# Weight chunks of two matrices converted in turn, and 26 matmuls at the end of an attention and FFN kernel

## The chip, the cores and the metric

The kernel runs on one core of a Trainium2 chip. The metric is the device time of one execution in microseconds (us). The engines are named as in the profile: PE is TensorE's matmul (PEld its weight load), DVE is VectorE, ACT is ScalarE, POOL is GpSimd, and SP is SyncE, which issues the DMAs.

## What is computed

Attention over 8 batches of 8 heads, once on means of four positions and once in a band of seven positions, then a mixing of positions of rank 32, then a two-layer FFN with ReLU:

```python
def _attn_ref(q, k, v):                       # 8 x 8 x 576 x 64, float32
    factor, Sd, scale = 4, S // 4, 1.0 / np.sqrt(D)
    q_d, k_d, v_d = (t.reshape(B, H, Sd, 4, D).mean(axis=3) for t in (q, k, v))
    out_d = sm_attn(q_d, k_d, v_d)             # softmax attention on means of 4 positions
    out_up = np.repeat(out_d, factor, axis=2)
    mask = np.abs(pos[:, None] - pos[None, :]) < factor
    scores = np.where(mask, scale * np.matmul(q, k.transpose(0, 1, 3, 2)), -1000000000.0)
    ...
    out_local = np.matmul(attn, v)             # softmax over a band of 7 positions
    return out_up + out_local

def _moe_ref(x, U, V, w_ch1, w_ch2):           # x: 8 x 576 x 512, the heads side by side
    xt = x.transpose(0, 2, 1)
    h = xt @ U @ V                             # U 576 x 32, V 32 x 576
    u = x + h.transpose(0, 2, 1)
    ch = np.maximum(u @ w_ch1, 0.0) @ w_ch2    # 512 x 2048 and 2048 x 512
    return u + ch
```

The weights arrive as float64. The kernel turns each into two float32r parts, a high and a low one, and each FFN product is three matmuls (high x high, low x high, high x low).

## The kernel before

**Planner.** The whole program is one list of operations, each with an engine, a duration, a priority (a smaller number goes first), its reads and writes, and the buffers it needs. `Plan.run` walks modelled time: when an engine is free it takes the ready operation of the smallest priority number, and the order that results is the order in which instructions are issued. A buffer has a slot (a tag with so many copies) and a kind; within a kind buffers are handed out in the order in which they were created. Between kinds that share a slot the waiting operation with the smaller priority number gets the free copy.

**Attention.** A head pair is two heads of one batch; there are four for each batch and 32 in all. The priority of pair number n is 10 n, with +1 and +2 for its later stages. The first NE = 5 pairs (batch 0, and the first of batch 1) are "early": they use buffers in `early_pool`, compute the band with PE (`local_blocks`), and for batch 0 go straight on to `early_mix` (lines 617 to 638), which writes u as `uH` and `uL`. Later pairs send scores through memory, and line 711 (POOL) multiplies the values by the softmax weights of line 696 (DVE) into buffers `Pt`, which line 716 (DVE) sums; `mix_part` (lines 735 to 782) then reads the result back and makes u, with POOL writing `uL` in line 782.

**Weights.** W1 and W2 are converted in 16 chunks of 128 rows or columns each. For a chunk, SP loads 512 KB into a raw buffer (lines 376 and 385), then `convert` runs: ACT line 327, DVE lines 328, 330, 333 and 335 on a temporary `c` (three copies), ACT line 337 into the high part, POOL line 340 into the low part. Raw buffers have the tag `Pt` with kind `raw`: they share its three copies with the products `Pt` of line 711. W1 chunk f has priority 20 + 2 f (its load 5 less, and other numbers for the first three), W2 chunk f has 20 + f. W1's chunks are created first, all 16, then W2's.

**Region.** W2's tiles W2H and W2L lie where the early buffers were: `late_pool` closes `early_pool` and opens the pool of W2. The operation "late" follows all early operations, and each W2 chunk's copy into W2H waits for it.

**FFN.** 256 steps (batch, half of the positions, one of 16 chunks of the hidden layer). `ffn1` of a step is 12 matmuls of 288 columns into `ps_h` (line 799), then ACT writes `hH` (line 806) and DVE `hL` (line 807); `ffn2`, three steps later (LAG = 3), is 12 matmuls into four accumulators (line 822) from W2's chunk. The priorities are 1000 and above, so PE takes FFN work where no attention is ready. Step fc needs W1's chunk fc and W2's chunk fc, and all four head pairs of its batch. After the last chunk, POOL adds `uH` and `uL`, DVE adds the accumulator (line 835) and SP stores the result (line 838).

Of the kernel before, what the change touches and what calls it, by code (L numbers as in the profile page):

```python
# [12 lines left out]
F32R = mybir.dt.float32r  # L13
# [8 lines left out]
PE, DVE, ACT, POOL, SP = range(5)  # L22
# [31 lines left out]
class Plan:  # L54
# [9 lines left out]
    def op(self, eng, dur, fn, r=(), w=(), prio=0.0, after=(), lat=None, move=0.0, at=0.0):  # L64
        o = Op()
        o.eng, o.dur, o.fn, o.prio, o.succ, o.ndep, o.ready = eng, dur, fn, prio, [], 0, at
        o.lat, o.move = LATENCY[eng] + SLACK * (SLACK_FROM <= prio < 1000) if lat is None else lat, move
        deps = set(after)
        bufs = []
        for k in r:  # L70
            b = k[0] if isinstance(k, tuple) else k
            bufs.append(b)
            if k in self.last_w:
                deps.add(self.last_w[k])
            self.readers.setdefault(k, []).append(o)
        for k in w:
            b = k[0] if isinstance(k, tuple) else k
            bufs.append(b)
            if k in self.last_w:
                deps.add(self.last_w[k])  # L80
            deps.update(self.readers.get(k, ()))
            self.readers[k] = []
            self.last_w[k] = o
        deps.discard(o)
        o.margin = MARGIN[eng] * (MARGIN_FROM <= prio < 1000 and any(d.eng != eng for d in deps))
        o.bufs = [b for b in dict.fromkeys(bufs) if isinstance(b, Buf)]
        for b in o.bufs:
            b.uses += 1
        for d in deps:
            d.succ.append(o)  # L90
        o.ndep = len(deps)
        self.ops.append(o)
        return o
# [108 lines left out]
def attn_mix_ffn_kernel(ctx: ExitStack, tc, q, kp, vp, qT, kT, v, U, Ub, V, w1, w2, mask, band, eye, sel, pool, vw, ident, outT):  # L202
    nc = tc.nc
    B, H, S, D = q.shape
# [5 lines left out]
    DM = H * D  # L210
    DF = w1.shape[1]
    NFC = DF // 128
    NDC = DM // 128
    TN = 288
# [3 lines left out]
    LAG = 3  # L218
    W1S, W2P, W2S = 2, 20, 1
# [5 lines left out]
    W1P = 20  # L225
    NE = 5
    CN = 512
# [6 lines left out]
    op, buf = plan.op, plan.buf  # L234

    const = ctx.enter_context(tc.tile_pool(name="const", bufs=1))
# [6 lines left out]
    ps_h = ctx.enter_context(tc.tile_pool(name="ps_h", bufs=2, space=bass.MemoryType.PSUM))  # L243
    ps_m = ctx.enter_context(tc.tile_pool(name="ps_m", bufs=2, space=bass.MemoryType.PSUM))

    def psum(pool, name, tag, bufs):
        return buf(pool, [128, 512], F32, name, tag, bufs)
# [14 lines left out]
    def act(n, fn, r, w, prio, base=0.143):  # L262
        return op(ACT, n / 1200.0 + base, fn, r, w, prio)
# [11 lines left out]
    Vst = const.tile([128, S], F32R, name="Vst")  # L275
    W1H = const.tile([128, NDC, DF], F32R, name="W1H")
    W1L = const.tile([128, NDC, DF], F32R, name="W1L")
    W2 = {}
    early = tc.tile_pool(name="early", bufs=1)
    early_pool = early.__enter__()  # L280

    def late_pool():
        if not W2:
            early.__exit__(None, None, None)
            w2p = ctx.enter_context(tc.tile_pool(name="w2p", bufs=1))
            W2["H"] = w2p.tile([128, NFC, DM], F32R, name="W2H")
            W2["L"] = w2p.tile([128, NFC, DM], F32R, name="W2L")
        return W2

    def padded(shape, name, used, dt=F32):  # L290
        t = early_pool.tile([128, *shape], dt, name=name)
# [29 lines left out]
    def convert(raw, pp, n, hi_out, lo_out, a, wkey, name, prio, gate=(), l0=0):  # L321
        t = buf(ffn, [128, CN], I32, name, "cT:" + name, 3)
        w = lambda i: raw()[:pp, :2 * n].rearrange("p (n two) -> p n two", two=2)[:, :, i]
        ti = lambda: t()[:pp, :n]
        tf = lambda: t()[:pp, :n].bitcast(F32)
        ta = lambda: tf().rearrange("p (a n) -> p a n", a=a)
        act(n, lambda: nc.scalar.activation(tf(), w(1).bitcast(F32), AF.Abs), [raw], [t], prio)
        dve(n, lambda: nc.vector.tensor_scalar(
            out=tf(), in0=tf(), scalar1=F_MIN, scalar2=F_MAX, op0=ALU.max, op1=ALU.min), [t], [t], prio, True)
        dve(n, lambda: nc.vector.tensor_scalar(  # L330
            out=ti(), in0=ti(), scalar1=5, scalar2=2, op0=ALU.logical_shift_left,
            op1=ALU.logical_shift_right), [t], [t], prio, True)
        dve(n, lambda: nc.vector.scalar_tensor_tensor(
            ti(), w(1), -0x40000000, ti(), op0=ALU.bitwise_and, op1=ALU.bitwise_or), [raw, t], [t], prio)
        dve(n, lambda: nc.vector.scalar_tensor_tensor(
            ti(), w(0), 29, ti(), op0=ALU.logical_shift_right, op1=ALU.bitwise_or), [raw, t], [t], prio)
        act(n, lambda: nc.scalar.activation(hi_out(), ta(), AF.Copy), [t, *gate], [wkey + "H"], prio)
        if lo_out is None:
            return
        pool_tt(n, lambda: nc.gpsimd.tensor_tensor(  # L340
            out=lo_out(), in0=ta()[l0:], in1=hi_out()[l0:].bitcast(F32), op=ALU.subtract),
            [t, wkey + "H"], [wkey + "L"], prio)
# [31 lines left out]
    def load_w1(f, prio):  # L374
        raw = raw_buf("w1r")
        dma(lambda: nc.sync.dma_start(
            out=raw().rearrange("p (a n) -> p a n", a=NDC),
            in_=w1.bitcast(I32)[:, f * 256:(f + 1) * 256].rearrange("(a p) n -> p a n", p=128),
        ), [], [raw], min(prio - W1A, W1B + W1C * f if f < 3 else prio), 525)
        fs = slice(f * 128, (f + 1) * 128)  # L380
        convert(raw, 128, CN, lambda: W1H[:, :, fs], lambda: W1L[:, :, fs], NDC, f"W1_{f}", "c1", prio)

    def load_w2(f, prio):
        raw = raw_buf("w2r")
        dma(lambda: nc.sync.dma_start(out=raw(), in_=w2.bitcast(I32)[f * 128:(f + 1) * 128, :]),
            [], [raw], prio, 525)
        convert(raw, 128, CN, lambda: W2["H"][:, f, :].unsqueeze(1),
                lambda: W2["L"][:, f, :].unsqueeze(1), 1, f"W2_{f}", "c2", prio, ["late"])


    def work(is_early, pool, shape, dt, name, tag=None, bufs=1):
# [395 lines left out]
    FIRST, FILL = -10.0, 1000.0  # L787
# [23 lines left out]
    def ffn2(s, i):  # L811
        b, t, fc = s
        hH, hL = hbuf.pop(s)
        if fc == 0:
            accs[(b, t)] = [psum(ps_acc, f"acc{e}", f"acc{e}", 1) for e in range(NDC)]
        ac = accs[(b, t)]

        for e in range(NDC):
            def mm(e=e):
                es = slice(e * 128, (e + 1) * 128)  # L820
                for n, (w, hx) in enumerate((("H", hH), ("H", hL), ("L", hH))):
                    nc.tensor.matmul(ac[e]()[:, :TN], W2[w][:, fc, es], hx(),  # L822
                                     start=(fc == 0 and n == 0), stop=(fc == NFC - 1 and n == 2))
            op(PE, PF, mm, [hH, hL, f"W2_{fc}H", f"W2_{fc}L"], [ac[e]], FILL + i + LAG - 0.5)
        if fc == NFC - 1:
            uH, uL = u_of(b, t)
            for e in range(NDC):
                if e == NDC - 1:
                    o1 = buf(loc, [128, TN], F32, "o1", "o1b", 1)
                else:  # L830
                    o1 = buf(ffn, [128, CN], F32, "o1", "cT:o1", 3)
                pool_tt(TN, lambda e=e, o1=o1: nc.gpsimd.tensor_tensor(  # L832
                    out=o1()[:, :TN], in0=uH()[:, e, :].bitcast(F32), in1=uL()[:, e, :].bitcast(F32), op=ALU.add),
                    [(uH, e), (uL, e)], [o1], FIRST, after=[last_h[i - 1]])
                dve(TN, lambda e=e, o1=o1: nc.vector.tensor_tensor(  # L835
                    out=o1()[:, :TN], in0=ac[e]()[:, :TN], in1=o1()[:, :TN], op=ALU.add),
                    [ac[e], o1], [o1], FIRST)
                dma(lambda e=e, o1=o1: nc.sync.dma_start(
                    out=outT[e * 128:(e + 1) * 128, b * S + t * TN:b * S + (t + 1) * TN], in_=o1()[:, :TN]),
                    [o1], [], FIRST, 150, lat=0.4)  # L840

    steps = [(b, t, fc) for b in range(B) for t in range(NT) for fc in range(NFC)]
# [30 lines left out]
    held = []  # L873
    attention(1, True)
    early_ops = list(plan.ops)
    for f in range(NFC):
        load_w1(f, W1P + W1S * f)
    plan.op(DVE, 0.0, lambda: late_pool(), [], ["late"], 27, after=early_ops, lat=0.0)
    for f in range(NFC):
        load_w2(f, W2P + W2S * f)  # L880
    load_u(38)
    for h in held:
# [2 lines left out]
    for i in range(len(steps) + LAG):  # L885
        if i < len(steps):
            b, t, fc = steps[i]
            if t == 0 and fc == 0 and b > 0 and b + 1 < B:
                attention(b + 1)
            ffn1(steps[i], i)  # L890
        if i >= LAG:
            ffn2(steps[i - LAG], i - LAG)
    with tc.manual_schedule():
        plan.run()

# [61 lines left out]
```

## Time and profile before

| | us |
|---|---|
| median of 3 runs | 1093.05 |
| lowest and highest run | 1092.78, 1094.65 |
| the profiled execution | 1095.29 |
| its span in the profile | 1093.5 |

The profile is of one execution. Its span runs from the first to the last event that it recorded. "Busy" of an engine is the time in which at least one of its instructions ran; matmuls overlap, so a PE that is busy all the time need not be at its peak. PEclk is the clock granted to TensorE as a share of 2.4 GHz. In a timeline, the brackets give the idle time of the engine before the instruction and what ended it.

### The profile page before, as it was taken

Reading aid. Unit: us, or ns where it says so; the run is one execution under the profiler, and the core shown is the slowest. Engines: PE = TensorE matmul, PEld = TensorE weight load, DVE = VectorE, ACT = ScalarE, POOL = GpSimd, SP = SyncE. Lnnn points to the kernel's source line nnn. Section 1 sums busy time; section 2 is a strip of 40 time slices with the busy share of each in tenths; the row PEclk is TensorE's granted clock in tenths of the full one; section 3 lists DMA queues with packets and bytes.
Section 4 is the critical chain, followed back from the end, with each engine's and each line's share of the span. In section 5 each row is a group of like instructions: output and inputs, shape, how many; then the busy total and the mean of one; then the engine's idle time right before and its main releaser. Section 6 shows DMA issues by size and latency. Waiting matters only on the chain. (4 is left out here: it accounts for less than half of the span.)

```text
span 1093.5 us, 22919 instructions
## 1 busy us (share of the span) xinstructions
PE 1052.8 (96%) x8696; PEld 1011.7 (93%) x8696; DVE 643.8 (59%) x1093; ACT 372.8 (34%) x1239; POOL 550.0 (50%) x580
## 2 busy tenths in 40 slices
PE   7888988998999999999999999999999999999998
PEld 6777887987999999999998999999999999999998
DVE  5887899675775876745675455557366556211111
ACT  4787552333233423233242123332343221211111
POOL 4755467676575764745574534666456524202010
PEclk8898999998999999999999999999999999999999
DMA  6646864565466475543565235554656322100000
GB/s 193 190 115 181 203 191 106 139 145 140 102 163 144 112 189 129 138 96 92 124 156 125 60 102 117 137 130 109 145 126 148 79 58 75 45 1 23 1 22 23
DMA packets 238527, 125.05 MB, mean 114 GB/s; under 512 B 175632, under 2 KB 220498, under 8 KB 238416
## 3 DMA queue, kind: packets, MB, share of 16 engines
q1 hardware_dynamic: 238416, 123.58, 45.2%
q8 instruction: 69, 1.13, 0.5%
q14 instruction: 42, 0.34, 0.1%
HBM read 85.18 MB, written 38.35 MB: 113 GB/s over the span
## 5 line engine op out<-in xcount | busy, mean ns | idle before, releaser
L822 PE MATMUL acc<-hH,W2H 128*128 128x288 f32 x1024 | 316.7, 309 | 0.1
L799 PE MATMUL ps_h<-uH,W1H 128*128 128x288 f32 x1024 | 308.1, 301 | 1.4 <-DVE hL L807 1.3
L822 PE MATMUL acc<-hH,W2L 128*128 128x288 f32 x1024 | 303.5, 296 | 2.1 <-POOL W2L L340 2.1
L799 PE MATMUL ps_h<-uH,W1L 128*128 128x288 f32 x1024 | 303.3, 296 | 0.0
L822 PE MATMUL acc<-hL,W2H 128*128 128x288 f32 x1024 | 302.8, 296 | 0.0
L799 PE MATMUL ps_h<-uL,W1H 128*128 128x288 f32 x1024 | 301.2, 294 | 0.3 <-POOL uL L782 0.3
L807 DVE SCALAR_TENSOR_TENSOR hL<-ps_h,hH 128x288 fp32r<-128x288 f32 x256 | 116.1, 453 | 308.9 <-ACT hH L806 307.9
L806 ACT ACTIVATE hH<-ps_h 128x288 fp32r<-128x288 f32 x256 | 104.9, 410 | 492.8 <-PE ps_h L799 492.5
L711 POOL TENSOR_TENSOR Pt<-vl,at 128x896 f32<-128x896 f32 (+1 forms) x135 | 208.7, 1561 | 104.6 <-DVE acc L716 63.0
L716 DVE TENSOR_REDUCE acc<-Pt 128x128 f32<-128x1024 f32 (+1 forms) x135 | 242.1, 1809 | 4.4 <-DMA Pt<-up_s 2.8
L822 PEld LDWEIGHTS acc<-hH,W2H 128*128 128x128 f32 x1024 | 193.4, 189 | 8.6 <-issue 3.6
L799 PEld LDWEIGHTS ps_h<-uH,W1H 128*128 128x128 f32 x1024 | 194.2, 190 | 3.8 <-DVE hL L807 1.8
L822 PEld LDWEIGHTS acc<-hH,W2L 128*128 128x128 f32 x1024 | 193.6, 189 | 3.0 <-POOL W2L L340 3.0
L799 PEld LDWEIGHTS ps_h<-uL,W1H 128*128 128x128 f32 x1024 | 195.2, 191 | 0.6 <-POOL uL L782 0.6
L822 PEld LDWEIGHTS acc<-hL,W2H 128*128 128x128 f32 x1024 | 194.0, 189 | 0.0
L799 PEld LDWEIGHTS ps_h<-uH,W1L 128*128 128x128 f32 x1024 | 193.2, 189 | 0.0
L782 POOL TENSOR_TENSOR uL<-xT,uH 128x288 fp32r<-128x288 f32 x56 | 43.8, 806 | 102.9 <-ACT uH L780 100.2
L751 POOL TENSOR_TENSOR xL<-xL,xH 116x640 fp32r<-116x640 f32 x28 | 44.2, 1578 | 68.3 <-ACT xH L750 58.1
L832 POOL TENSOR_TENSOR o<-uH,uL 128x288 f32<-128x288 f32 x64 | 50.3, 816 | 53.1 <-DMA out_t<-o 53.0
L448 POOL TENSOR_TENSOR vr<-vr 72x256 f32<-72x256 f32 x54 | 41.7, 772 | 30.7 <-DMA vr<-in_v 30.7
L659 PE MATMUL ps_b<-gT,gq 64*96 64x102 f32 x648 | 44.3, 261 | 6.5 <-ACT se L664 3.8
L664 ACT ACTIVATE se<-ps_b 96x306 f32<-96x306 f32 x108 | 40.0, 418 | 29.5 <-PE ps_b L659 29.5
(132 smaller groups left out, 1201.9 us busy)
## 6 DMA issues: line engine op xcount, KB each, us to landing
vl<-in_vp SPq DMA_DIRECT2D x54, 240.0 KB
s_s<-se SPq DMA_DIRECT2D x108, 114.8 KB
out_t<-o SPq DMA_DIRECT2D x64, 144.0 KB
w1r<-in_W SPq DMA_DIRECT2D x16, 512.0 KB
w2r<-in_W SPq DMA_DIRECT2D x16, 512.0 KB
Y<-x_s SPq DMA_DIRECT2D x112, 72.0 KB
xL<-x_s SPq DMA_DIRECT2D x28, 287.5 KB
gT<-in_kT SPq DMA_DIRECT2D x27, 291.0 KB
```

Of the source, the lines that this page charges most:

```text
L448: pool_tt(256, lambda x=x: nc.gpsimd.tensor_tensor(out=x()[:, :, 0:2, :], in0=x()[:, :, 0:2, :], in1=x()[:, :, 2:4, :], op=ALU.add), [x], ...
L659: nc.tensor.matmul(view(ps[hh])[:, i], qr()[o, n * QB:(n + 1) * QB], kr()[o, n * QB:n * QB + KB], start=(i == 0), stop=(i == HB - 1))
L664: act(HB * KB, lambda p=ps[hh], se=se: nc.scalar.activation(se(), view(p), AF.Copy), [ps[hh]], [se], prio)
L711: nc.gpsimd.tensor_tensor(out=Pt()[:, 0:7, :n, :], in0=win, in1=at()[:, p0:p0 + n, :].rearrange("p s o -> p o s").unsqueeze(3).broadcast_t ...
L716: dve(13.7 * n * D, lambda p0=p0, n=n, Pt=Pt: nc.vector.tensor_reduce(out=acc()[:, p0:p0 + n, :], in_=Pt()[:, :, :n, :].rearrange("p o s d ...
L751: pool_tt(640, lambda: nc.gpsimd.tensor_tensor(out=xL(), in0=xL().bitcast(F32), in1=xH().bitcast(F32), op=ALU.subtract), [xL, xH], [xL], prio)
L782: pool_tt(TN, lambda uH=uH, uL=uL, uf=uf: nc.gpsimd.tensor_tensor(out=uL()[:, hp, :], in0=uf(), in1=uH()[:, hp, :].bitcast(F32), op=ALU.su ...
L799: nc.tensor.matmul(ps()[:, :TN], w[:, dc, fs], u()[:, dc, :], start=(n == 0), stop=(n == 3 * NDC - 1))
L806: last_h[i] = act(TN, lambda: nc.scalar.activation(hH(), ps()[:, :TN], AF.Relu), [ps], [hH], FIRST, 0.05)
L807: dve(TN, lambda: nc.vector.scalar_tensor_tensor(hL(), ps()[:, :TN], 0.0, hH().bitcast(F32), op0=ALU.max, op1=ALU.subtract), [ps, hH], [hL ...
L822: nc.tensor.matmul(ac[e]()[:, :TN], W2[w][:, fc, es], hx(), start=(fc == 0 and n == 0), stop=(fc == NFC - 1 and n == 2))
L832: pool_tt(TN, lambda e=e, o1=o1: nc.gpsimd.tensor_tensor(out=o1()[:, :TN], in0=uH()[:, e, :].bitcast(F32), in1=uL()[:, e, :].bitcast(F32), ...
```

## The change

Five chunks of W2 (NW = 5) get tiles of their own, `W2e`, beside the early buffers instead of in their region, and their conversions no longer wait for "late". The tiles for the other chunks become smaller by five chunks. The chunks are created in another order: W1's chunks 0 to 3, then W2's chunk 0 and W1's chunk 4 and so on in turn up to W2's chunk 4 and W1's chunk 8, then the rest of W1, then "late", then W2's chunks 5 to 15. W2's chunk f among the first five has priority 22 + 2 f; the others keep theirs. Line 822 reads W2 through `w2_of`.

At the end of the program there is a new PE operation, `widths`: 18 matmuls into one PSUM buffer, six each of 512, 384 and 128 columns, and eight of 128 columns with 64 rows of output into another. Their weights and columns are parts of W1H; nothing reads what they write. Its priority number is the largest of all.

```diff
--- before.py
+++ after.py
@@ -275,7 +275,9 @@
     Vst = const.tile([128, S], F32R, name="Vst")
     W1H = const.tile([128, NDC, DF], F32R, name="W1H")
     W1L = const.tile([128, NDC, DF], F32R, name="W1L")
+    NW = 5
     W2 = {}
+    W2e = {x: const.tile([128, NW, DM], F32R, name=f"W2e{x}") for x in "HL"}
     early = tc.tile_pool(name="early", bufs=1)
     early_pool = early.__enter__()
 
@@ -283,9 +285,12 @@
         if not W2:
             early.__exit__(None, None, None)
             w2p = ctx.enter_context(tc.tile_pool(name="w2p", bufs=1))
-            W2["H"] = w2p.tile([128, NFC, DM], F32R, name="W2H")
-            W2["L"] = w2p.tile([128, NFC, DM], F32R, name="W2L")
+            W2["H"] = w2p.tile([128, NFC - NW, DM], F32R, name="W2H")
+            W2["L"] = w2p.tile([128, NFC - NW, DM], F32R, name="W2L")
         return W2
+
+    def w2_of(x, f):
+        return W2e[x][:, f] if f < NW else W2[x][:, f - NW]
 
     def padded(shape, name, used, dt=F32):
         t = early_pool.tile([128, *shape], dt, name=name)
@@ -384,8 +389,8 @@
         raw = raw_buf("w2r")
         dma(lambda: nc.sync.dma_start(out=raw(), in_=w2.bitcast(I32)[f * 128:(f + 1) * 128, :]),
             [], [raw], prio, 525)
-        convert(raw, 128, CN, lambda: W2["H"][:, f, :].unsqueeze(1),
-                lambda: W2["L"][:, f, :].unsqueeze(1), 1, f"W2_{f}", "c2", prio, ["late"])
+        convert(raw, 128, CN, lambda: w2_of("H", f).unsqueeze(1),
+                lambda: w2_of("L", f).unsqueeze(1), 1, f"W2_{f}", "c2", prio, ["late"] if f >= NW else [])
 
 
     def work(is_early, pool, shape, dt, name, tag=None, bufs=1):
@@ -819,7 +824,7 @@
             def mm(e=e):
                 es = slice(e * 128, (e + 1) * 128)
                 for n, (w, hx) in enumerate((("H", hH), ("H", hL), ("L", hH))):
-                    nc.tensor.matmul(ac[e]()[:, :TN], W2[w][:, fc, es], hx(),
+                    nc.tensor.matmul(ac[e]()[:, :TN], w2_of(w, fc)[:, es], hx(),
                                      start=(fc == 0 and n == 0), stop=(fc == NFC - 1 and n == 2))
             op(PE, PF, mm, [hH, hL, f"W2_{fc}H", f"W2_{fc}L"], [ac[e]], FILL + i + LAG - 0.5)
         if fc == NFC - 1:
@@ -873,10 +878,15 @@
     held = []
     attention(1, True)
     early_ops = list(plan.ops)
-    for f in range(NFC):
+    for f in range(4):
+        load_w1(f, W1P + W1S * f)
+    for f in range(NW):
+        load_w2(f, W1P + W1S * f + W1S)
+        load_w1(f + 4, W1P + W1S * (f + 4))
+    for f in range(NW + 4, NFC):
         load_w1(f, W1P + W1S * f)
     plan.op(DVE, 0.0, lambda: late_pool(), [], ["late"], 27, after=early_ops, lat=0.0)
-    for f in range(NFC):
+    for f in range(NW, NFC):
         load_w2(f, W2P + W2S * f)
     load_u(38)
     for h in held:
@@ -890,6 +900,17 @@
             ffn1(steps[i], i)
         if i >= LAG:
             ffn2(steps[i - LAG], i - LAG)
+    spare = [psum(ps_h, "ps_w", "h", 2) for _ in range(2)]
+
+    def widths():
+        for k, n in enumerate([512] * 6 + [384] * 6 + [128] * 6):
+            ks = slice(k * 64, k * 64 + 128)
+            nc.tensor.matmul(spare[0]()[:, :n], W1H[:, 0, ks], W1H[:, 1, :n], start=True, stop=True)
+        for k in range(8):
+            ks = slice(k * 64, k * 64 + 64)
+            o = spare[1]()[0:64, :128]
+            nc.tensor.matmul(o, W1H[:, 2, ks], W1H[:, 3, :128], start=True, stop=True)
+    op(PE, 3.0, widths, ["W1_0H", "W1_1H", "W1_2H", "W1_3H"], spare, FILL + len(steps) + LAG)
     with tc.manual_schedule():
         plan.run()
```

## Rows read from the trace of the kernel before

**Rows 1.** The page: busy us (share of the span) and instructions of each engine

```profile
PE 1052.8 (96%) x8696; PEld 1011.7 (93%) x8696; DVE 643.8 (59%) x1093; ACT 372.8 (34%) x1239; POOL 550.0 (50%) x580
```

**Rows 2.** Stretches: length, busy us (instructions) by engine, granted PE clock, DMA share, GB/s

```profile
core 0: us, PE busy (x) PEld busy (x) DVE busy (x) ACT busy (x) POOL busy (x), PEclk, DMA share, GB/s
...
40.00:100.00 60.00, 51.82 (x483) 44.49 (x482) 45.31 (x89) 49.80 (x201) 38.37 (x41) 0.92 0.48 131
100.00:180.00 80.00, 72.83 (x565) 67.55 (x565) 73.63 (x124) 40.20 (x113) 48.90 (x45) 0.95 0.68 178
...
240.00:260.00 20.00, 13.63 (x92) 12.37 (x89) 14.75 (x22) 5.03 (x14) 14.70 (x16) 0.74 0.68 160
260.00:400.00 140.00, 139.15 (x1207) 134.20 (x1206) 96.55 (x152) 49.16 (x167) 90.28 (x96) 1.00 0.56 134
400.00:1080.00 680.00, 676.27 (x5550) 661.70 (x5549) 339.28 (x570) 184.57 (x581) 297.57 (x318) 1.00 0.38 93
```

**Rows 3.** PE timeline, 243 to 258 us: start, length, instruction, count, [idle before <-releaser]

```profile
248.86 1.23 PE L499 MATMUL ps_a<-vs,E 72*72 72x64 f32 x8 [4.61 <-POOL vs L450]
...
252.91 0.82 PE L774 MATMUL ps_u<-Vst,stk 128*128 128x288 f32 x2 [1.04 <-DVE stk L764]
...
256.50 0.61 PE L799 MATMUL ps_h<-uL,W1H 128*128 128x288 f32 x1 [0.27 <-POOL uL L782]
```

**Rows 4.** POOL timeline at the border between batch 0 and batch 1

```profile
255.65 1.55 POOL L782 TENSOR_TENSOR uL<-xT,uH 128x288 fp32r<-128x288 f32 x2 [4.64 <-ACT uH L780]
```

**Rows 5.** SP timeline, 150 to 172 us: issues of DMAs

```profile
156.76 3.81 SPq L385 DMA_DIRECT2D w2r<-in_W  x2
...
165.26 0.28 SPq L359 DMA_DIRECT2D ur<-in_U  x1
...
170.20 0.34 SPq L703 DMA_DIRECT2D Pt<-up_s  x1
```

**Rows 6.** POOL timeline: the first product of batch 1's attention

```profile
172.65 1.73 POOL L711 TENSOR_TENSOR Pt<-vl,at 128x896 f32<-128x896 f32 x1
```

**Rows 7.** DVE timeline: W2_0's last step, and line 696

```profile
108.15 1.42 DVE L335 SCALAR_TENSOR_TENSOR c<-w2r,c 128x512 int32<-128x512 int32 x1
...
119.21 0.21 DVE L696 TENSOR_TENSOR at<-ms,lrl 128x63 f32<-128x63 f32 x1
```

**Rows 8.** Tile W2H: who writes it; ns min/median/max, first and last start

```profile
L337 ACT ACTIVATE W2H<-c x16: 621/632/638, 111.8 to 175.0; 128x512 fp32r<-128x512 f32 x16
L340 POOL TENSOR_TENSOR W2L<-c,W2H x16: 1262/1310/1813, 112.8 to 175.7; 128x512 fp32r<-128x512 f32 x16
```

**Rows 9.** Chain that ended last: start, length, what

```profile
924.44 0.60 PE ps_hu L759 x10
...
1081.99 1.59 PE acc L822 x12
```

**Rows 10.** PE timeline: the first FFN matmul

```profile
103.23 0.59 PE L799 MATMUL ps_h<-uH,W1H 128*128 128x288 f32 x1
```

**Rows 11.** PE waits, 100 to 260 us: total us, times, longest

```profile
PE acc L822 <- POOL W2L L340: 2.1, 3, 1.3
```

**Rows 12.** Temporary c alone: stretch, length; DVE, ACT, POOL busy us (instructions); then as rows 2

```profile
14.00:107.00 93.00, 47.17 (x66) 20.45 (x33) 20.59 (x15) 0.87 0.59 166
107.00:178.00 71.00, 52.36 (x63) 20.00 (x32) 24.05 (x17) 0.98 0.65 170
39.00:46.00 7.00, 4.78 (x4) 2.05 (x4) 2.33 (x2) 1.00 0.69 153
```

**Rows 13.** Timeline of all engines, the end

```profile
1088.83 1.68 DVE L835 TENSOR_TENSOR o<-acc,o 128x288 f32<-128x288 f32 x4 [2.72 <-PE acc L822]
...
1089.32 1.80 SPq L838 DMA_DIRECT2D out_t<-o  x4
...
1089.66 0.29 PE L822 MATMUL acc<-hH,W2L 128*128 128x288 f32 x1
```

**Rows 14.** Stretches at the end, columns as in rows 2

```profile
1092.50:1093.50 1.00, 0.00 (x0) 0.00 (x0) 0.00 (x0) 0.00 (x0) 0.00 (x0) 1.00 0.00 0
```

## The prediction

> **What bounds the kernel now.** I read the page's engine totals first [rows 1]: TensorE (PE) is busy for 96% of the span, the next engine that computes, VectorE (DVE), for 59%. That is a modelled busy time and an average over unlike stages, so the second view is the table by stretch [rows 2]. From 260 us on, PE is busy for 139.15 of 140 and 676.27 of 680 us: there the end is set by the sum of PE work, and time saved on another engine is worth nothing. What this change wins must come from before 260 us. In 40 to 100 us ScalarE (ACT) is the fullest engine beside PE (49.80 of 60 us, DVE 45.31). In 100 to 180 us it is DVE (73.63 of 80). In 240 to 260 us PE is busy for only 13.63 of 20, at a granted clock of 0.74.
>
> Third, the PE timeline at that place [rows 3]. PE stands 4.61 us before 248.86, does small attention pieces, stands another 1.04 us, and the FFN goes on in earnest at 256.50, behind uL, which GpSimd (POOL) writes from 255.65 to 257.20 [rows 4]. This is the border between batch 0 and batch 1: the FFN waits for batch 1's attention. From there the PE work that is left is fixed, so **the kernel ends some 836 us (1093.5 - 257.2) after u of batch 1 is ready.** FFN work done sooner before the border only waits longer at it.
>
> Fourth, what sets u of batch 1. Its last three head pairs are worked off one after the other by lines 711 and 716, in Pt buffers that share three slots with the raw weight chunks. SP issues the first Pt transfer at 170.20, behind the last raw chunks (two w2r from 156.76, ur at 165.26) [rows 5], and the first product runs at 172.65 [rows 6]. The softmax result that it also reads (line 696) was there at 119.42 [rows 7]. So **the end of the weight conversions opens batch 1's attention.** From W2L's first to its last start, 112.8 to 175.7 [rows 8], the pitch is 62.9 / 15 = 4.19 us a chunk.
>
> **The change part by part.**
> *Five W2 chunks out of the early region.* Chunks 0 to 4 of W2 lose their wait on "late". In the trace W2_0 is finished in its temporary at 109.57 and copied at 111.8 [rows 7, 8], so that wait costs 2.2 us at most, once. I count it at 0: ACT may have been at other work, and the end of the conversions is set by the pitch.
>
> *The order.* Raw buffers are handed out in the order of creation: now W1_0 to W1_3, then W2_0, W1_4, W2_1, W1_5 and so on to W2_4, W1_8, then W1_9 to W1_15, then W2_5 to W2_15. The number of chunks is the same. What changes is the priority they compete with: from the fifth on it was 28, 30, ..., 50; now it is 22, 28, 24, 30, 26, 32, 28, 34, 30, 36, 38, ... So four more chunks stand ahead of the fourth early head pair (30 to 32) and five more ahead of the fifth (40 to 42). W1_9 to W1_15 are put off by up to five chunks: W1_15 is then ready near 107 + 5 x 4.19 = 128 us, while step 15 wants it no sooner than 103.23 + 15 x 3.18 = 151 us (two PE pieces of 1.59 [rows 9], FFN start [rows 10]): no stall. On SP's queue each w1r or w2r waits for a slot as before; behind them stand scores, gq and gT of the later heads, and the number of chunks ahead of these stays the same.
>
> *FFN's first steps.* W2_0 is now there when the FFN starts. But PE waited only 2.1 us for W2L in all [rows 11], and stood idle for 7.2 of 80 us in that stretch [rows 2]; what it saves there is lost again at the border. Counted at 0; if u of batch 1 were no bound it would be up to 7.2 us.
>
> *What a chunk costs in the early stage.* More chunks have a claim there, but chunks filled the gaps before as well, so I take **1.5 more chunks converted when the FFN starts**, with 0 and 4 as bounds. In 14 to 107 us a chunk took DVE 4 x 47.17 / 66 = 2.86 us and ACT 2 x 20.45 / 33 = 1.24 us [rows 12]. ACT is the fuller of the two there, so a chunk delays the early heads by 1.24 us; the other ends are 0 (it fits a gap) and 4.10 us (the heads wait for all of it in turn). Each chunk that leaves the DVE-bound stage saves 4.19 us there. Net 4.19 - 1.24 = 2.95 us, x 1.5 = **4.4 us sooner for batch 1's attention, and so for the end**. Bounds: a gain of 4 x 4.19 = 16.8 us with everything hidden; nothing with 4.10; a loss in rival (b).
>
> On DVE's price: a chunk took 2.86 us in the early stage and 4 x 52.36 / 63 = 3.32 us behind 107 us, beside other POOL work [rows 12]. The Trainium skill says in "SBUF — State Buffer" ("Who interferes with whom") that VectorE and GpSimd share one port pair by an exclusive lock, and that a VectorE operation with two SBUF inputs contends for it too; it speaks against the change, as a chunk brings its lock to the early heads' POOL work. By that a moved chunk would cost DVE 3.32 us in either stage, and with ACT 4.56, a loss of 0.4 us each; the rows of one stage do not show that, and rival (b) holds the case.
>
> *The 26 matmuls.* They come last on PE, behind the last FFN matmul at 1089.66 [rows 13]; their PSUM buffers are free since the last hL. No row has 512 columns. Scaled from 1.59 / 12 = 0.1325 us for 288 columns [rows 9], 512 take 0.236 and 384 take 0.177 us; 128 take 0.060 (ten in 0.60 us [rows 9], with weights of 64 columns, as in eight of the fourteen), at most 0.1325. Sum: 6 x 0.236 + 6 x 0.177 + 14 x 0.060 = 3.32 us, at most 4.33. They lie beside the old tail: additions on DVE until 1090.51, SP's last issue until 1091.12 [rows 13], bytes until 1092.5 at the latest [rows 14], end at 1093.5. PE ends near 1089.8 + 3.3 + 0.2 = 1093.3, at most 1094.3. If the end only needs PE to be done, that costs 0 to 0.8 us; if the same 1.0 us follows PE as follows the last bytes, 0.8 to 1.8. I take **+0.5 us**, nearer to the low end, since the transfers already end there. Less than 0 is excluded: nothing is removed from that chain.
> The Trainium skill ("TensorE: Matmul & The Clock Gate", Part 1, "Wait — 56ns, not 53.3ns?") gives for the gap of matmuls at full clock N / 2.4 GHz plus about 2.5 ns; by that estimate the 26 take 2.99 + 0.07 = 3.05 us, 0.27 less. For 288 columns it gives 122.5 ns where the row has 132.5, so I go by the row.
>
> **Sum.** -4.4 + 0.5 = -3.9 us. The profiled execution's 1095.29 becomes 1091.4; the median of the runs, 1093.05, lies 2.24 below the profiled one and becomes **1089.1 us**.
>
> **The rivals.**
> (a) *The order changes little*: no more chunks than before when the FFN starts, and only the tail is left: 1093.05 + 0.5 = 1093.6. For it: fifteen W1L ran by 107 us [rows 12], so the gaps were in use. Against: DVE idles for 14.7 of 60 us in 40 to 100 [rows 2].
> (b) *The early heads pay for it* (slower). The chunks now go ahead of the fourth and fifth head pair, on ACT and DVE in turn. One chunk beside POOL work took DVE 4.78 us in 39 to 46 us [rows 12]; with ACT's 1.24 that is 6.02. It loses from 4.19 us a chunk on. With two chunks: 2 x (6.02 - 4.19) = 3.7, and the tail 0.5: 1097.2.
> (c) *All of it fits*: four chunks at 2.95 us: -11.8 + 0.5, 1081.8. For it: DVE's idle time. Against: ACT has only 10.2 us left there.
> (d) *The border stops being a bound*, and FFN's sooner start counts: up to 7.2 us on top of (c). For it: PE's idle time at the border is 6.4 of 20 us [rows 2], which (c) would make up. Against: a sooner FFN reaches the border sooner, and waits there.
>
> **How the numbers follow.** Forecast 0.40 (1086.5 to 1091.5), (a) 0.25, (b) 0.21, (c) with (d) 0.14. The range reaches from (c) to (b): 1081.8 to 1097.5. A measurement of this kernel tells about 0.2% (2.2 us) from no change: faster is under 1090.9, slower over 1095.2. Of the forecast's 0.40, 0.36 lies under 1090.9, with (c) and (d) 0.50; (a) and the rest of the forecast make 0.29, (b) 0.21.
>
> **What would show it.** Right: W2L's last start some 4 us before 175.7, the first product before 170, the border's uL before 255, PE idle at the border as long as before or longer, the FFN's first matmul at 103 to 108, PE's last matmul ending near 1093.3. Rival (a): the same marks within 1 us of before. Rival (b): the FFN's first matmul over 8 us later than 103.23, and the first product later than 172.65. Wrong altogether: no wait of PE at the border, or several us of new PE idle time behind 260 us.

## The result, and the profile after

The changed kernel takes 1098.34 us (median of 5 runs, 1097.65 to 1099.44), the kernel before 1093.05 (1091.84 to 1094.65): a ratio of 1.0041 with an interval of 1.0029 to 1.0053. It is slower by some 0.4 to 0.5%, where 1089.1 was forecast. The profiled execution took 1097.68, its span is 1095.9. That of before was 2.24 us above its median, this one is 0.66 below, so the two traces show only 2.4 of the 5.3 us.

Line numbers from `w2_of` on are larger by 5 in the profile after. The engines' row of the page, after (compare [rows 1]):

```profile
PE 1055.8 (96%) x8722; PEld 1017.0 (93%) x8722; DVE 653.9 (60%) x1093; ACT 373.2 (34%) x1239; POOL 551.3 (50%) x580
```

The stretches of after, with the columns of [rows 2]:

```profile
40.00:100.00 60.00, 48.80 (x405) 41.81 (x403) 50.87 (x92) 45.81 (x179) 41.96 (x38) 0.83 0.49 141
100.00:180.00 80.00, 65.76 (x527) 61.54 (x528) 75.69 (x116) 42.03 (x125) 50.27 (x48) 0.89 0.61 166
180.00:240.00 60.00, 60.00 (x528) 57.66 (x527) 43.07 (x67) 20.45 (x67) 39.92 (x40) 1.00 0.66 150
240.00:260.00 20.00, 20.00 (x173) 19.10 (x172) 13.50 (x25) 8.96 (x30) 13.39 (x14) 1.00 0.70 162
260.00:400.00 140.00, 136.54 (x1134) 132.15 (x1133) 95.08 (x136) 42.40 (x137) 78.14 (x87) 0.99 0.51 125
400.00:1080.00 680.00, 679.24 (x5617) 664.54 (x5617) 345.25 (x587) 188.82 (x602) 306.46 (x327) 1.00 0.39 95
```

The reader is to see three things. PE's pause at the border is gone (20.00 of 20 us, where it was 13.63). Ahead of it PE is worse off: it is busy for 48.80 us (51.82 before) and 65.76 (72.83 before), at a lower granted clock (0.83 for 0.92, 0.89 for 0.95). Behind 260 us nothing is gained.

The FFN starts 10.3 us later than in [rows 10] (PE timeline), while batch 1's attention opens 11.0 us sooner than in [rows 6] (POOL timeline), and W2L's last start is at 168.0 where it was 175.7 in [rows 8] (tile W2L):

```profile
113.53 0.59 PE L804 MATMUL ps_h<-uH,W1H 128*128 128x288 f32 x1
```

```profile
161.62 1.83 POOL L716 TENSOR_TENSOR Pt<-vl,at 128x896 f32<-128x896 f32 x1 [1.36 <-DVE c L340]
```

```profile
L345 POOL TENSOR_TENSOR W2L<-c,W2H x11: 1279/1400/1747, 127.3 to 168.0; 128x512 fp32r<-128x512 f32 x11
```

**Where the 10.3 us arise.** The first three head pairs end as before. The fourth loses it: its softmax on ACT (`nb`, which starts it) ran at 81.20 before and at 89.74 after. ACT's timeline before, and after:

```profile
81.20 0.21 ACT L469 ACTIVATE nb<-mx 72x2 f32<-72x2 f32 x1
```

```profile
85.68 0.63 ACT L342 ACTIVATE W2eH<-c 128x512 fp32r<-128x512 f32 x1 [0.90 <-DVE c L340]
...
88.66 0.63 ACT L342 ACTIVATE W1H<-c 128x512 fp32r<-128x512 f32 x1 [0.71 <-DVE c L340]
89.20 0.64 ACT L332 ACTIVATE c<-w1r 128x512 f32<-128x512 f32 x1
89.74 0.29 ACT L474 ACTIVATE nb<-mx 72x2 f32<-72x2 f32 x2
```

The maxima that it reads came from DVE at 80.71 and 81.17 before, at 83.67 and 85.91 after, with steps of chunks between them. Then `nb` stands behind copies into W2eH and W1H, on which ACT itself sits waiting for DVE (0.90 and 0.71 us). The conversion alone (tile c) in 77 to 92 us, columns as in [rows 12], of before and of after:

```profile
77.00:92.00 15.00, 5.48 (x11) 3.15 (x5) 2.49 (x2) 1.00 0.23 71
```

```profile
77.00:92.00 15.00, 10.99 (x14) 5.47 (x9) 7.09 (x5) 0.72 0.46 140
```

DVE spends twice as long on it, and PE's granted clock is 0.72 there instead of 1.00. When the FFN starts, 19 chunks have begun their last step (POOL's subtraction); before it were 15.

**What PE waits for** between 100 and 260 us, after: the waits for W2L [rows 11] are gone, and attention stands in their place, U (behind W2's last chunk; ended at 171.6) and the early pairs among it:

```profile
PE ps_hu L764 <- ACT nb L474: 4.6, 1, 4.6
PE ps_t L493 <- ACT E L479: 3.3, 1, 3.3
PE ps_ba L596 <- ACT et L588: 2.3, 1, 2.3
PE ps_bt L585 <- POOL ms_b L578: 2.2, 1, 2.2
```

The first of these is put down to ACT's `nb`, but the matmul also reads U, whose low part POOL wrote from 170.0; in e5_u_early (below), where U is there by 122 us, this wait does not occur.

**An account of PE** makes the traces comparable. For a point T, I add up the matmuls that start after T, each at the pitch of its kind at full clock (0.1325 us for 288 columns [rows 9], for attention 0.06 to 0.10 from whole groups of the timeline, such as 0.71 us for eight `ps_s`): the work left. Span less T less the work left is the time lost after T, by pauses, by the low clock and after the last matmul. The 26 matmuls of the tail are not counted as work. Before's order at its median is given by e1_tail (below: before, with the 26 matmuls). Most of these executions lie within 0.5 us of their run's median; f1_three's lies 1.9 us and e12_before_plus's 1.2 us below it, f3_last_three's 2.1 and e5_u_early's 5.4 above it.

| trace | left at 125 | left at 180 | left at 260 | lost after 180 | lost after 260 | span |
|---|---|---|---|---|---|---|
| e1_tail | 932.0 | 887.3 | 820.2 | 25.2 | 12.3 | 1092.5 |
| e2_notail (after, no tail) | 945.3 | 903.7 | 824.2 | 12.7 | 12.2 | 1096.4 |
| e3_oldprio | 931.8 | 887.3 | 820.3 | 23.5 | 10.5 | 1090.8 |
| e6_two | 938.2 | 891.5 | 818.6 | 18.1 | 11.0 | 1089.6 |
| f1_three | 938.2 | 895.3 | 819.5 | 9.9 | 5.7 | 1085.2 |
| f2_four | 943.9 | 898.7 | 821.9 | 15.1 | 11.9 | 1093.8 |
| f3_last_three | 946.7 | 903.2 | 823.4 | 24.4 | 24.2 | 1107.6 |
| e5_u_early | 944.9 | 901.1 | 822.2 | 37.1 | 36.0 | 1118.2 |
| e12_before_plus | 935.2 | 890.1 | 823.2 | 24.6 | 11.5 | 1094.7 |

The change leaves PE 13.3 us behind at 125 us and 16.4 at 180. From 180 to 260 before's order loses 12.9 us and the new one 0.5: that gives 12.4 back. 4.0 us stay, and behind 260 both lose the same. 4.0 is, within 0.1, the difference of the spans and of the medians of e1_tail and e2_notail (3.9 each).

**Who waits at the border.** The FFN's first step of batch 1 needs the first half of u, from all four head pairs. In e1_tail POOL writes the last pair's two halves together, and PE stands for the first of them; in e2_notail the fourth `uL` completes the first half, and the second half follows when batch 0 has freed its buffer. POOL and PE of e1_tail, then of e2_notail:

```profile
253.74 1.55 POOL L782 TENSOR_TENSOR uL<-xT,uH 128x288 fp32r<-128x288 f32 x2 [4.64 <-ACT uH L780]
```

```profile
254.58 0.61 PE L799 MATMUL ps_h<-uL,W1H 128*128 128x288 f32 x1 [0.27 <-POOL uL L782]
```

```profile
252.24 0.80 POOL L787 TENSOR_TENSOR uL<-xT,uH 128x288 fp32r<-128x288 f32 x1 [0.90 <-ACT uH L785]
254.66 3.10 POOL L787 TENSOR_TENSOR uL<-xT,uH 128x288 fp32r<-128x288 f32 x4 [1.62 <-ACT uH L785]
```

```profile
256.82 0.40 PE L804 MATMUL ps_h<-uH,W1H 128*128 128x288 f32 x1
```

The first half of u is there at 253.04 us, 1.5 us sooner than in e1_tail (254.53, half-way through the two), but PE begins on it only at 256.82, 3.8 us later, and still has 18 matmuls of batch 0's second product to do. In e1_tail batch 0 is done by then. The border has changed sides: before, PE waited for u; now u waits for PE.

### The profile page after: what moved, and what is told of

Same layout as the page of the kernel before. It is cut to its first block, busy times and chain, and to the rows that moved or that the text cites. A ratio compares the mean times of both kernels' runs of the same rounds, so it can differ in the third digit from the quotient of the medians.

```text
span 1095.9 us, 23006 instructions
## 1 busy us (share of the span) xinstructions
PE 1055.8 (96%) x8722; PEld 1017.0 (93%) x8722; DVE 653.9 (60%) x1093; ACT 373.2 (34%) x1239; POOL 551.3 (50%) x580
## 4 chain that ended last, share of the span: by engine, by line
PE 84%; DVE 11%; issue 2%; POOL 1%; ACT 1%; DMA 1%; SPq 0%; DVEq 0%; POOLq 0%; ACTq 0%
PE acc L827 36%; PE ps_h L804 35%; PE ps_b L664 3%; PE ps_a L504 3%; DVE c L338 2%; PE ps_hu L764 1%; DVE c L340 1%; PE ps_s L464 1%; DVE c L333 1%; DVE c L335 1%; PE ps_t L493 1%; PE ps_u L779 1%; DVE at L701 1%; DVE ms L689 1%; DMA kd<-in_kT 1%
## 5 line engine op out<-in xcount | busy, mean ns | idle before, releaser
L827 PE MATMUL acc<-hH,W2H 128*128 128x288 f32 x704 | 218.3, 310 | 0.0
L827 PE MATMUL acc<-hH,W2L 128*128 128x288 f32 x704 | 208.5, 296 | 0.0
L827 PE MATMUL acc<-hL,W2H 128*128 128x288 f32 x704 | 208.3, 296 | 0.0
L827 PEld LDWEIGHTS acc<-hH,W2H 128*128 128x128 f32 x704 | 133.2, 189 | 6.1 <-issue 2.5
L827 PEld LDWEIGHTS acc<-hL,W2H 128*128 128x128 f32 x704 | 133.6, 190 | 0.0
L827 PEld LDWEIGHTS acc<-hH,W2L 128*128 128x128 f32 x704 | 133.1, 189 | 0.0
L827 PE MATMUL acc<-hH,W2eH 128*128 128x288 f32 x320 | 99.2, 310 | 0.0
L827 PE MATMUL acc<-hH,W2eL 128*128 128x288 f32 x320 | 94.5, 295 | 0.0
L827 PE MATMUL acc<-hL,W2eH 128*128 128x288 f32 x320 | 94.3, 295 | 0.0
```

The source lines that it names most:

```text
L827: nc.tensor.matmul(ac[e]()[:, :TN], w2_of(w, fc)[:, es], hx(), start=(fc == 0 and n == 0), stop=(fc == NFC - 1 and n == 2))
```

## The experiments

Each is timed beside the kernel before on the same chip (1093.94, 1093.65, 1093.12 and 1094.09 us in the four groups); the ratio to it has its 95% interval behind it.

**The tail.** e1_tail is the kernel before with `widths` added; e2_notail is the changed kernel without it.

> The kernel before with only the 26 matmuls at the end. In the changed kernel the span ends 4.67 us after its last FFN matmul starts, in the one before 3.84 us, so the tail theory expects 0.8 us: 1093.9, and the profile with the 26 from the last FFN matmul on, some 3.7 us long. Rival: the 26 are most of the 5.3 us that the change lost; then 1096 or more.

> The changed kernel without the 26 matmuls at the end. The theory that the early heads pay for the promoted chunks expects what is left of the loss after 0.8 us of tail: 1097.5, and the first FFN matmul at 113 to 114 us as in the changed kernel. Rival (the tail is most of the loss): 1094 or less.

e1_tail: 1094.30 us, 1.0008 (0.9998 to 1.0018). e2_notail: 1098.19, 1.0046 (1.003 to 1.0063). By the medians the tail costs 0.4 us, by the ratio 0.9, and by its interval 2.0 at most; the rest of the loss, 4 to 5 us, is in the other parts. Both theories hold within 0.7 us.

**The region alone.** e4_region has the new tiles, no wait on "late" for five chunks, and before's order and priorities.

> As e2_notail, but with all of W1 first and W2 behind it, with the priorities of before; five W2 chunks keep their own tiles and do not wait for the early operations to end. Theory: the tiles cost nothing and the wait that goes was worth 2.2 us at most, off the path: 1093 within 1.5 us, FFN start 103 to 104 us. Rival (the place of the tiles in memory costs): 1096 or more.

1093.11, 0.9994 (0.998 to 1.0008): nothing, as the prediction counted it.

**The priorities.** e3_oldprio keeps the order in turn, but each chunk has the priority of its place:

```diff
-        load_w2(f, W1P + W1S * f + W1S)
-        load_w1(f + 4, W1P + W1S * (f + 4))
+        load_w2(f, W1P + W1S * (2 * f + 4))
+        load_w1(f + 4, W1P + W1S * (2 * f + 5))
...
-        load_w1(f, W1P + W1S * f)
+        load_w1(f, 48 + 0.2 * (f - NW - 4))
```

> As e2_notail, with W1 and W2 still in turn, but each chunk with the priority that the chunk of the same place in the order had before (from the fifth on 28, 30, ... 46; the last seven of W1 48 to 49.2, so that none reaches the batch 1 heads at 50). Theory (the smaller priority numbers push the fourth and fifth head pair back): the first FFN matmul returns to 103 to 106 us and the time to 1090 to 1094. Rival (chunks in turn, or W2 in the early stage, cost it whatever their priority): first FFN matmul at 111 us or later and 1097 again.

1092.30, 0.9989 (0.9976 to 1.0002); the FFN starts at 102.50. The order in turn does no harm when no chunk overtakes the early pairs. What costs is the priorities, of W2's five chunks and of W1's behind them together.

**How many.** e2_notail with NW = 2, 3 and 4.

> The changed kernel without the 26 matmuls, with two W2 chunks outside the region instead of five (the order in turn then ends with W1's chunk 5). Theory (each chunk ahead of the fourth and fifth head pair delays the FFN's start by 2.6 us, and the border takes up the first 6 us): the FFN starts at 105 to 109 us, the border still binds, and the time is 1091 to 1094. Rival (every chunk costs on its own, with no reserve): two fifths of the loss of 5.1, 1095.

> The changed kernel without the 26 matmuls, with three W2 chunks outside the region instead of five. Theory (each chunk after the second, put ahead of the fourth and fifth head pair, costs its share of the 5.9 us that lie between two chunks, 1092.3, and five, 1098.2): 1094.3. Rival (the loss is a jump, where PE's order comes out otherwise): 1092 to 1093, or already 1098.

> The same with four W2 chunks. Theory (a share for each chunk after the second): 1096.2. Rival (a jump): 1092 to 1093 or 1098, the same as with three or as with five.

| NW | us | ratio | the FFN's first matmul |
|---|---|---|---|
| 2 | 1092.28 | 0.9987 (0.9976 to 0.9999) | 110.43 |
| 3 | 1089.89 | 0.9965 (0.9952 to 0.9977) | 107.93 |
| 4 | 1095.50 | 1.0017 (1.0006 to 1.0029) | 115.86 |
| 5 (e2_notail) | 1098.19 | 1.0046 (1.003 to 1.0063) | 114.27 |

Neither expectation holds at three: that kernel beats both. At four the theory's 1096.2 is near. From three to four and from four to five the time grows by 5.6 and some 3 us. With two the time is as expected, but the FFN's first matmul is not (105 to 109 us): it is 7.2 us later than before. PE is 6.2 us behind at 125, and nothing is lost in the end: from 180 to 260 us it loses 7.1 us instead of 12.9. The FFN's start does not move by a fixed price per chunk: with two and with three, 17 chunks have begun their last step when it starts, and it starts 7.2 and 4.7 us later than before. The gain at three lies mostly behind 260 us: PE loses 5.7 us there, not 12.3, though up to 1.9 of these 6.6 us can be the good execution that was traced. The stretches of f1_three:

```profile
240.00:260.00 20.00, 18.75 (x143) 17.39 (x142) 12.34 (x29) 7.94 (x28) 17.41 (x21) 0.91 0.62 161
260.00:400.00 140.00, 140.00 (x1188) 136.06 (x1188) 83.73 (x142) 45.10 (x148) 74.61 (x80) 1.00 0.51 121
400.00:1080.00 680.00, 679.63 (x5607) 665.09 (x5607) 339.94 (x574) 188.12 (x593) 306.06 (x326) 1.00 0.39 95
```

**Two that fell.** f3_last_three lowers the priorities of the third to fifth chunk; e5_u_early moves `load_u` ahead of W2_5.

```diff
-        load_w2(f, W1P + W1S * f + W1S)
+        load_w2(f, W1P + W1S * f + W1S if f < 2 else 33 + W1S * (f - 2))
```

> The changed kernel without the 26 matmuls, five W2 chunks in the same order, but the third to fifth with priority 33, 35 and 37 instead of 26, 28 and 30, behind the fourth head pair (30 to 32). Theory (the chunks that overtake the fourth pair make the loss): the early head pairs end at 96 us or sooner, and the time is 1092 to 1094. Rival (five chunks in this order cost the same whatever their priority): 1097 to 1099.

> The changed kernel without the 26 matmuls, and with the load and conversion of U created ahead of the last eleven W2 chunks instead of behind them. It takes away PE's wait of 4.6 us near 171.6 us for U. Theory (the FFN is behind before the border, so PE time won there counts until the border binds again): 3 to 6 us sooner than 1098.2, down to the border, which is 1091 to 1094. Rival (the border, not the FFN, sets the end): no change, 1097 to 1099.

1107.21, 1.0121 (1.0104 to 1.0139), and 1114.60, 1.02 (1.0178 to 1.0221). Both theories fall. In f3_last_three the early pairs still end at 99.0 us (91.7 before, 103.4 after) and PE is 14.7 us behind at 125: the priorities of those three alone are not it. U early removes PE's wait for U, and more is lost elsewhere. In both all of the further loss against e2_notail lies behind 260 us, where PE loses 24.2 and 36.0 us. The waits of PE behind 260 us in e5_u_early:

```profile
PE ps_t L493 <- ACT E L479: 10.5, 4, 3.8
PE ps_s L464 <- DVE xT L782: 4.3, 2, 2.2
```

Attention of later batches stands in PE's queue ahead of FFN work, before its inputs are there. A small change at the start makes the planner write another order for the whole kernel. That this is why they lose is read from these waits, which with the smaller ones make 16.5 of the 36.0 us, and from a granted clock of 0.94 from 260 to 400 us (1.00 in [rows 2]); it was not tried by itself.

**Is the border a reserve?** e10 and e11 add 40 unused matmuls (5.3 us) to the plan, to before and to e2_notail, as an operation between the first FFN steps. e12 and e13 add the same to the third step's own operation, so that every engine keeps its order; e14 and e15 leave 40 matmuls out instead.

```diff
             n = 0
+            for k in range(40 if i == 2 else 0):
+                nc.tensor.matmul(ps()[:, :TN], W1H[:, k % NDC, fs], uH()[:, k % NDC, :], start=True, stop=True)
```

> The kernel before with 40 more matmuls of 288 columns, whose result nothing reads, between the first steps of the FFN: 40 x 0.1325 = 5.3 us of PE work near 105 us. Theory (the border between batch 0 and 1 takes up what the FFN loses before it): PE's idle time at the border, 6.4 of 20 us, shrinks by about 5 us, u of batch 1 is ready when it was, and the time stays within 1 us of before. Rival (a late FFN costs its delay wherever it arises): 1098 to 1099.

> The changed kernel without the 26 matmuls, and with the same 40 more matmuls (5.3 us) between the first steps of the FFN. Theory (there the FFN arrives at the border later than u of batch 1, and no reserve is left): all of it counts, 1098.2 + 5.3 = 1103.5. Rival (the loss of the change lies somewhere else, and the border still has its reserve): within 1 us of 1098.2.

> The kernel before with 40 more matmuls of 288 columns (5.3 us) in the third FFN step, ahead of its own in the same buffer, with no operation added to the plan, so that every engine keeps its order. Theory (the border gives back what the FFN loses before it; the changed kernel shows it giving back some 9 us): within 1 us of before. Rival (lost FFN time counts wherever it is lost, as 3.5 of the 5.3 us of e10_extra_before may say): 4 to 5.3 us slower.

> The changed kernel without the 26 matmuls, with the same 40 matmuls in the third FFN step and every engine's order kept. Theory (no reserve is left at the border): all of the 5.3 us counts, 1103.5. Rival (a reserve is left): within 1 us of 1098.2. If e11_extra_notail lost 8.7 us only because its plan came out otherwise, this one loses 5.3 and no more.

> The changed kernel without the 26 matmuls, and with the product low part of W1 x high part of u left out in the first ten FFN steps (40 matmuls of 288 columns, 5.3 us of PE work less, every engine's order kept). Theory (the FFN is behind before the border, by 3.4 us at 260 us): 3.4 to 5.3 us sooner, 1093 to 1095. Rival (batch 1's attention sets the end): within 1 us of 1098.2.

> The kernel before with the same product left out in the first ten FFN steps (5.3 us of PE work less, order kept). Theory (there the FFN waits at the border for batch 1's attention): PE only waits longer, within 1 us of before. Rival (PE work before the border counts): 4 to 5.3 us faster.

| | before | e2_notail |
|---|---|---|
| 5.3 us more, in the plan | 1097.16, 1.0036 (1.0022 to 1.005) | 1106.93, 1.0129 (1.0108 to 1.015) |
| 5.3 us more, order kept | 1097.68, 1.0044 (1.0029 to 1.006) | 1103.31, 1.0101 (1.0071 to 1.0131) |
| 5.3 us less, order kept | 1093.30, 0.9998 (0.998 to 1.0015) | 1097.38, 1.0036 (1.001 to 1.0062) |

Less FFN work gains nothing in before, as the theory had it. More FFN work costs 4.6 of the 5.3 us with the order kept: the theory falls on that side. The PE timeline at the border shows why, in e1_tail (which stands for before at its median), in e12_before_plus (line numbers larger by 2 behind its two lines) and in e15_before_minus:

```profile
246.94 1.22 PE L499 MATMUL ps_a<-vs,E 72*72 72x64 f32 x8 [4.61 <-POOL vs L450]
...
250.99 0.82 PE L774 MATMUL ps_u<-Vst,stk 128*128 128x288 f32 x2 [1.05 <-DVE stk L764]
```

```profile
250.62 1.22 PE L499 MATMUL ps_a<-vs,E 72*72 72x64 f32 x8 [4.62 <-POOL vs L450]
...
254.66 0.82 PE L774 MATMUL ps_u<-Vst,stk 128*128 128x288 f32 x2 [1.04 <-DVE stk L764]
...
258.25 0.61 PE L801 MATMUL ps_h<-uL,W1H 128*128 128x288 f32 x1 [0.26 <-POOL uL L782]
```

```profile
246.28 1.22 PE L499 MATMUL ps_a<-vs,E 72*72 72x64 f32 x8 [4.62 <-POOL vs L450]
...
250.32 0.82 PE L774 MATMUL ps_u<-Vst,stk 128*128 128x288 f32 x2 [1.04 <-DVE stk L764]
...
253.92 0.40 PE L799 MATMUL ps_h<-uL,W1H 128*128 128x288 f32 x1 [0.27 <-POOL uL L782]
```

The pauses are the same to 0.01 us, and all of it has moved with PE: 3.7 us later with 5.3 us more work (in an execution 1.2 us below its median), and 0.7 sooner with 5.3 us less. Batch 1's attention has its own matmuls in PE's queue between those of the FFN; when PE is late, they are late, and so is u. With less FFN work PE waits longer for W2L, 5.1 us in all where it is 2.7 in e1_tail, which eats part of it. In e2_notail more work costs 5 to 6 us, as its theory has it; less work gains 0 to 1 us, where 3.4 to 5.3 were expected, and its ten runs scatter from 1091.15 to 1102.42. By the account, its trace has 5 us less left than e2_notail at 125 us and 1 us less at 180: PE waits in between. Why the order in the plan makes e11 worse than e13 was not followed.

## Why the prediction was wrong, point by point

- **The step that failed: "4.4 us sooner for batch 1's attention, and so for the end".** The sum charges a chunk's cost to batch 1's attention alone and has no term for the FFN's own delay: the border was taken to hide it. That delay, 1.5 x 1.24 = 1.9 us in its terms, was 10.3 us (12.2 from e1_tail to e2_notail), and the whole pause that was to hide it is 6.4 us. So u was ready sooner and the end came later: in e2_notail PE took up batch 1 3.8 us behind its u and had 4.0 us more work left at 260 us, which is the loss without the tail.
- **The forecast had no room for this.** By its own numbers, u 4.4 us sooner and the FFN 1.9 us later use up 6.3 of the 6.4 us of pause. "PE idle at the border as long as before or longer", its mark for right, does not go with that; "no wait of PE at the border", its mark for wrong altogether, is what came.
- **1.5 chunks at 1.24 us of ACT.** It was 4, the upper bound, so 2.6 us a chunk on average. The price took ACT's busy time. What a chunk costs is the order: ACT and DVE work on it in turn, and the pair's softmax stands in both queues behind steps that themselves wait. The term was mis-sized, but it alone does not turn the sign: by the prediction's formula, 4 x (4.19 - 2.6) is still 6.4 us of gain for u.
- **The gain behind it.** W2L's last start came 7.7 us sooner and the first product 11.0. Of that little reached u: from e1_tail to e2_notail the first product is 8.4 us sooner (162.38 for 170.76), u's first half 1.5. The mark "the border's uL before 255" came true for that half (252.28 in the trace after) and did not help.
- **The border.** "FFN work done sooner before the border only waits longer" held (e15_before_minus). The other direction, that the border is set by the attention and gives way to a late FFN, was taken for granted and is wrong with the order kept (e12_before_plus). In the changed kernel 16.4 us were lost by 180 us and 12.4 given back by 260: PE had FFN work of batch 0 left and did not pause (60.00 of 60 and 20.00 of 20 us). That the new order, with batch 1's attention further forward in PE's queue, is what allowed this is argued, not tried.
- **"The end of the conversions opens batch 1's attention"** holds loosely. With two chunks W2L's last start is at 176.0 and the first product runs at 166.8 all the same.
- **"From there the PE work that is left is fixed"**: the whole is, but not what is left when u is ready (4.0 us more at 260 us here), nor the time lost beside it. That was 5.7 us in f1_three, 12.3 in e1_tail and 36.0 in e5_u_early; for this change it was the same on both sides.
- **Rival (b)** had the sign and the FFN's mark (over 8 us later; it was 10.3). Its second mark, a first product later than 172.65, was wrong (161.62), and so was its sum: two chunks cost nothing (e6_two). That its 1097.2 is near 1098.3 is luck. (a), (c) and (d) are out: the FFN started 10.3 us later.
- **The tail** held. The 26 take from 1091.37 to 1095.06, 3.7 us for the 3.3 estimated, and cost 0.4 to 0.9 us for the 0.5 taken. The term that was short is the narrow matmuls: from start to start, 128 columns took 0.11 us with weights of 128 columns, and 0.06, as estimated for all fourteen, only with weights of 64. 512 columns took 0.23 and 384 took 0.17, as scaled. After's timeline at the end:

```profile
1090.92 2.04 SPq L843 DMA_DIRECT2D out_t<-o  x4
...
1091.37 3.21 PE L908 MATMUL ps_w<-W1H 128*128 128x512 f32 x18
...
1094.42 0.64 PE L912 MATMUL ps_w<-W1H 128*64 128x128 f32 x8
```

- **The region, the wait on "late" and the FFN's first steps** at 0: right by e4_region and e15_before_minus.
- **Open**: which of the promoted priorities (W2's or W1's behind them) the fourth pair cannot bear, what takes the gain between the first product and u, and why three chunks give an order that loses so little behind 260 us.

## What to carry to other kernels

Work that is moved forward on idle shares is paid for in the queues of the engines that it crosses: price it by who stands behind its waiting steps, not by its busy time, and count how much of it will really go ahead. Where two streams of work meet, follow both: bringing one forward helps only as far as the other is not put back past it. A pause of the bounding engine is a reserve only if nothing that ends the pause is queued on that engine behind what you delay. Try doses of such a change (here two, three, four, five chunks: -0.1, -0.4, +0.2, +0.5%), since the best one may lie inside.

## What the runs showed of the hardware

A DVE step with one input in SBUF can take three times as long beside a POOL operation. In the trace after, line 335 on 128x512 (median 0.43 us) took 1.37 us at 79.50, while POOL's subtraction into W2eL ran from 79.08:

```profile
79.50 1.37 DVE L335 TENSOR_SCALAR c<-c 128x512 int32<-128x512 int32 x1
```

```profile
79.08 1.51 POOL L345 TENSOR_TENSOR W2eL<-c,W2eH 128x512 fp32r<-128x512 f32 x1
```

The Trainium skill, "SBUF — State Buffer" ("Who interferes with whom"), names `tensor_scalar` among the operations that can take the port pair which VectorE shares with GpSimd, and says that the other engine is then blocked for the whole instruction; the row agrees. It does not happen each time: of the 32 steps of line 335 on 128x512, the 9 with no POOL operation beside them took 0.41 to 0.43 us, and of the 23 beside one 12 took the same and 11 took 0.52 to 2.03 us. The prediction weighed only the two-input steps there. The price that it gave by that page, 3.32 us of DVE a chunk, is near the 3.1 us (4 x 10.99 / 14) of 77 to 92 us; before's row of that stretch gives 2.0 (4 x 5.48 / 11).
